# Spectral and gated mix on one core: first loads on one queue, shorter warm-up matmuls, and products in another order with PSUM pairs begun by ScalarE

## Chip, cores and metric

The kernel runs on one core of one Trainium2 chip. The metric is the device time of one execution in microseconds (us). The kernel before took 802.03 us, the median of three runs (801.37 to 802.43).

TensorE (PE) does the matmuls, VectorE (DVE) and ScalarE (ACT) the elementwise work. SyncE (SP) issues loads and GpSimd (POOL) issues stores; each issues on a DMA queue of its own, and the transfers of all queues share the core's 16 DMA engines. PSUM, the memory that TensorE writes into, is used as 8 banks of 128 x 512 fp32; a pair of banks holds one product of 128 x 1024.

## What is computed

```python
x = A_x                                               # (1, 2048, 512), fp32
g = sigmoid((x * gate_w).sum(-1, keepdims=True))
a  = einsum("ts,bse->bte", Cr, x @ Wr.T) - einsum("ts,bse->bte", Ci, x @ Wi.T)   # FNet
gate, up = x @ W_gate, x @ W_up                       # to 1792 columns
b  = (gate * (gate > 0) * up) @ W_down                # ReGLU
return g * a + (1 - g) * b
```

`Cr` and `Ci` (2048 x 2048) and `Wr` and `Wi` (512 x 512) are the real and imaginary parts of Fourier matrices. They come as inputs and are multiplied like any others.

## The kernel before

**Products.** Every large product is cut into 2 x 2 blocks and done with seven block products instead of eight, after Strassen. `LEFT` and `RIGHT` (lines 25 to 28) say which sums of blocks each of the seven multiplies, `ORDER` (29) in which order, and `BANK` (30) in which pair of PSUM banks. fp32 operands are split into a high and a low part in fp32r, so each block product is three matmuls per slice of 128: low by high, high by low, high by high (`PARTS`, 375). `hi_of` (398, ScalarE) makes a high part (the profile's casts into `ch`, `lh`, `xh`), `lo_of` (401, VectorE) the low one (`cl`, `ll`, `xl`).

**Stages, in TensorE's order.**
- Warm-up matmuls (950 to 958): 8 of 128 x 512 on a constant tile.
- `Direct` (544): the first block of gate and up, 96 matmuls in eight plain products, fed as its first loads land.
- 11 gated blocks, `Block` (491): gate and up for two of F's 128-column tiles and half of the rows. Seven products of 12 matmuls, in two banks of 6 each: 84.
- 4 `SpectralBlock`s (655) of 84 for x by Wr and Wi, two for each half of the rows, then two more gated blocks (the tail).
- Rounds (`Round`, 766) into the tiles named `z`: 2 of `Down` (843; 294 matmuls each) for W_down, and 4 of `Sequence` (865; 336 each) for Cr and Ci, of which the last is `Last` (904).

That makes 3456 matmuls after the warm-ups, nearly all of 512 columns. Intermediate results go to DRAM and come back: `hd` (gated blocks, stored by `h_out` with the sums that the next stage needs), `ad` (spectral blocks), `vd` and `zd` (rounds), `lb` (the prepared left operands of ci's two rounds), `wb` (the weights of c = 1, kept for the tail).

**What sets the order of the work.** The class `Plan` (129). Each piece of work is recorded with a key, counted in matmuls of the stream: `op(plan.now - 90, load, ...)` asks for something 90 matmuls before the current place. `due` (182) works out by when each step must be done, `order` (196) then places the steps greedily on each engine: TensorE, SyncE and GpSimd in the order of their keys, VectorE and ScalarE by due time, no sooner than 40 keys ahead (`AHEAD`, 139). `run` (262) maps every buffer onto one of 51 SBUF units of 4 KB per partition (`UNITS`); a unit is given again when its last reader is done, so a new buffer can make its first writer wait for an engine or a store that has nothing else to do with it. PSUM tiles come from a rotation of 8 single banks (`bank`, 336; `Pair`, 339), and a new tile waits for all users of the eighth before it. All instructions are issued by line 126 (`Step.run`), so the trace has that one line for all and groups are told apart by tile names.

**The evacuation of a gated block** (`Block.evac`, 515). After each bank: product 5 is copied by ScalarE from pair a into `t`; VectorE adds product 2 (pair b) to `t`, then subtracts `t` from product 1 (pair c). Products 3 and 4 accumulate onto pairs a and b, which still hold 5 and 2: ScalarE's relu of the first bank into `g`, VectorE's product with the second into `h`. Products 6 and 7 accumulate further; VectorE adds `t` to each bank (`u`), and one scalar_tensor_tensor makes max(u, 0) times the other. `SpectralBlock.evac` (680) has the same form without the relu. A round evacuates by `Round.evac` (811), which copies products 1 and 5 (`u`, `n5`) and then combines banks on VectorE (`w`, `u2`).

**The start** (960 to 988). `Direct` needs half of x's tile 11 and half of its weights `wf` for its first product. The weights (two tiles in two halves, 256 KB each) are issued by SyncE (`load`), x's four halves of 256 KB by ScalarE (`side`, 366); the other x tiles and the weights of c = 1 follow on SyncE. `x_split` and `w_split` make the high and low parts of each half.

**The last round.** `Last.prepare` (907) multiplies the earlier partial result `z` by the gate, adds it to `v` and stores it to `vd`, four times, 24 keys apart, with 8 loads and 4 stores of 512 KB. It begins 150 keys after the second of the four sequence rounds began (`start`, 1063). `Last.end` (935) scales the last product's banks by the gate, adds them to `v` and stores each bank.

**The loads of a sequence round** (`Sequence.rights`, 874): for each quarter jj four tiles `r` of 512 KB from cr or ci, asked for 90 keys before their first use; sums of them in place; then `split` (786) casts them into `ch` and `cl`, 31 and 24 keys ahead of the product.

Of the kernel before, what the change touches and what calls it, by code (L numbers as in the profile page):

```python
# [128 lines left out]
class Plan:  # L129
# [30 lines left out]
    def read(self):  # L160
# [3 lines left out]
        seen, banks = {}, []  # L164
        for s in self.steps:
            for refs, writes in ((s.reads, False), (s.writes, True)):
                for r in refs:
                    old = seen.setdefault(r.base, [])
                    for box, x, w in old:
                        if x is not s and (w or writes) and meet(box, r.box):  # L170
                            s.after.add(x)
                    if writes:
                        old[:] = [o for o in old if not within(o[0], r.box)]
                    old.append((r.box, s, writes))
                    if not r.base.uses and r.base.kind == "bank":
                        banks.append(r.base)
                    r.base.uses.append(s)

        for old, new in zip(banks, banks[8:]):
            new.uses[0].after.update(x for x in old.uses if x is not new.uses[0])  # L180
# [81 lines left out]
    def run(self, nc, unit, bank):  # L262
# [5 lines left out]
        for b in self.bufs:  # L268
            if b.uses and b.kind in ("unit", "bank"):
# [3 lines left out]
        for n, s in enumerate(self.steps):  # L273
            for b in first.get(n, ()):
                if b.kind == "bank":
                    b.tile = bank(b)
                    continue
# [9 lines left out]
def kernel(ctx: ExitStack, tc, xP, xG, wf, wgu, wd, cr, ci, wri, gw, out):  # L287
# [19 lines left out]
    psum = ctx.enter_context(tc.tile_pool(name="psum", bufs=8, space=PSUM))  # L307
# [28 lines left out]
    def bank(b):  # L336
        return psum.tile([P, N], F32, name=b.name, tag="ps")

    class Pair:


        def __init__(self, name):
            self.name, self.banks = name, None

        def new(self):
            self.banks = [Buf(plan, self.name, [N], kind="bank") for _ in range(2)]

        def __getitem__(self, n):
            return self.banks[n].all
# [15 lines left out]

    def side(o, i):
        plan.scalar.dma_start(o, i)
# [19 lines left out]
    def x_raw(q, m):  # L387

        a, *r = RIGHT[m]
        raw = piece[q, {6: "12", 7: "21"}[m] if m in (6, 7) else a] if not r or m in (6, 7) else buf(f"xs{m}")  # L390
        X[q, m] = buf(f"xh{m}", dtype=F32R), buf(f"xl{m}", dtype=F32R), raw

    def x_sum(q, m):
        a, *r = RIGHT[m]
        if r:
            combine(X[q, m][2].all, piece[q, a].all, piece[q, r[0]].all, r[1])
# [15 lines left out]
    SLOT = {5: 0, 1: 1, 2: 2, 4: 0, 3: 1, 7: 2, 6: 3}  # L412

    class Weights:
        def __init__(self, c):
            self.c = c
            self.raw = [buf(f"wr{i}", [4, 2, P]) for i in range(2)]
            self.sum = [buf(f"ws{i}", [3, 2, P]) for i in range(2)]
# [6 lines left out]
        def a_sum(self, i):  # L425
            r, o = self.raw[i], self.sum[i]
            E().vector.tensor_add(o[:, 0], r[:, 1], r[:, 2])
            E().vector.tensor_add(o[:, 1], r[:, 0], r[:, 1])
            E().vector.tensor_add(o[:, 2], r[:, 0], r[:, 3])
            E().scalar.copy(self.a[i][0].all, o.all)  # L430

        def a_lo(self, i):
            E().vector.tensor_sub(self.a[i][1].all, self.sum[i].all, f32(self.a[i][0].all))

        def b_sum(self, i):
            r = self.raw[i]
            E().vector.tensor_sub(r[:, 2:4], r[:, 2:4], r[:, 0:2])

        def b_hi(self, i):
            E().scalar.copy(self.b[i][0].all, self.raw[i].all)  # L440

        def b_lo(self, i):
            E().vector.tensor_sub(self.b[i][1].all, self.raw[i].all, f32(self.b[i][0].all))
# [11 lines left out]
        def of(self, m, i):  # L455
            return [t[:, SLOT[m]] for t in (self.a if m in (5, 1, 2) else self.b)[i]]

    def w_prep(w, key, ahead=66):
        for i in range(2):
            op(key - ahead + 6 * i, w.load, i)  # L460
            op(key - 36 + 12 * i, w.a_sum, i)
            op(key - 30 + 12 * i, w.a_lo, i)
            op(key + 6 * i, w.b_sum, i)
            op(key + 6 * i, w.b_hi, i)
        op(key + 6, w.b_lo, 0)
        op(key + 12, w.b_lo, 1)
# [24 lines left out]
    class Block:  # L491


        def __init__(self, q, w):
            self.q, self.w = q, w
            self.t, self.g, self.u = buf("t"), buf("g"), buf("u")
            self.h = [buf(f"h{d}") for d in range(2)]
            self.ps = {k: Pair("c") for k in "abc"}
            for m in ORDER:
                for i in range(2):  # L500
                    pe(6, self.product, m, i)
                    self.evac(m, i, plan.now)
            h_out(q, w.c, self.h, plan.now + (8 if plan.now > 270 else 100))

        def product(self, m, i):
            w, x, ps = self.w.of(m, i), X[self.q, m], self.ps[BANK[m]]
            if m in (5, 2, 1) and i == 0:
                ps.new()
            n = 0
            for k in range(2):  # L510
                for a, b in PARTS:
                    mm(ps[i], w[a][:, k], x[b][:, k], start=m in (5, 2, 1) and n == 0, stop=n == 5)
                    n += 1

        def evac(self, m, i, key):
            a, b, c = (self.ps[k] for k in "abc")
            t, g, h = self.t, self.g, self.h

            def go():
                e = E()  # L520
                if m == 5:
                    e.scalar.copy(t[:, i], a[i])
                elif m == 2:
                    e.vector.tensor_add(t[:, i], t[:, i], b[i])
                elif m == 1:
                    e.vector.tensor_sub(t[:, i], c[i], t[:, i])

                elif m in (3, 4):
                    j, ps = (0, a) if m == 3 else (1, b)
                    if i == 0:  # L530
                        e.scalar.activation(g[:, j], ps[0], AF.Relu)
                    else:
                        e.vector.tensor_mul(h[0][:, 1] if m == 3 else h[1][:, 0], g[:, j], ps[1])
                else:
                    j, ps, o = (0, a, h[1][:, 1]) if m == 6 else (1, b, h[0][:, 0])
                    u = self.u[:, j] if i == 0 else o
                    e.vector.tensor_add(u, ps[i], t[:, i])
                    if i:
                        e.vector.scalar_tensor_tensor(o, self.u[:, j], 0.0, o, op0=OP.max, op1=OP.mult)

            op(key, go)


    class Direct:
        def __init__(self):
# [6 lines left out]
            self.ps = {(f, j): Pair("c") for f in range(2) for j in range(2)}  # L552
# [17 lines left out]
        def products(self, all):  # L570
            for d, i, f, j, k, n in all:
                first = d == k == n == 0
                if first and i == 0:
                    self.ps[f, j].new()
# [4 lines left out]
        def w_load(self, d, k=slice(0, 2)):  # L579
            load(self.raw[d][:, k], wf[d, :, k])  # L580

        def w_split(self, d, k=slice(0, 2)):
            hi, lo = self.w[d]
            E().scalar.copy(hi[:, k], self.raw[d][:, k])
            E().vector.tensor_sub(lo[:, k], self.raw[d][:, k], f32(hi[:, k]))
# [51 lines left out]
    class Spectral:  # L637
# [8 lines left out]
        def prep(self, m, key):  # L646
            a, *r = LEFT[m]
            raw = self.raw[a] if not r or m in (6, 7) else buf(f"vs{m}")
            w = self.w[m] = buf(f"vh{m}", dtype=F32R), buf(f"vl{m}", dtype=F32R), raw
            if r:  # L650
                op(key, lambda: combine(raw.all, self.raw[a].all, self.raw[r[0]].all, r[1]))
# [3 lines left out]
    class SpectralBlock:  # L655
        def __init__(self, sp, q, ih):
            self.sp, self.q, self.ih = sp, q, ih
            self.t = buf("t")
            self.o = {b: buf("a" + b, (2, 2, HD)) for b in ("12", "21", "22", "11")}
            self.ps = {k: Pair("a") for k in "abc"}  # L660
            for m in ORDER:
                for i in range(2):
                    pe(6, self.product, m, i)
                    op(plan.now, self.evac, m, i)
                if m in (3, 4, 6, 7):
# [462 lines left out]
```

## Time and profile before

| | kernel before |
|---|---|
| median of three runs | 802.03 us |
| span of the profiled execution | 799.7 us |
| TensorE busy | 790.3 us, 99%, 3464 matmuls |
| weight loads (beside the matmuls) | 652.1 us, 82% |
| VectorE busy | 665.6 us, 83%, 791 instructions |
| ScalarE busy | 329.1 us, 41%, 393 instructions |
| GpSimd busy | 91.7 us, 11%, 146 instructions |
| moved by DMA | 192.79 MB, mean 241 GB/s |

The times come from other executions than the profile, so the span is compared with the span of another profile, and the median with a median. "Busy" is a share of the whole span and says nothing about who waits for whom: that stands in the rows of single waits. In those, "[5.22 <-DMA r<-ci]" means that the engine had been idle for 5.22 us and that a load into a tile r from ci released it. A row of the timeline gives start, duration, engine, operation, the tiles as out<-in, and the sizes; "x4" means that four such instructions in a row are folded together. A row of the windows gives the stretch, then the busy time and instructions of PE, weight loads, VectorE, ScalarE and GpSimd, the granted TensorE clock, the mean busy share of the DMA engines, and GB/s. An engine's name with a q (SPq, POOLq) is its sequencer, where DMAs are issued; the number at the end of a DMA row is the median time from issue to landing.

### The profile page before, as it was taken

The numbers are of one execution on the slowest core, as the hardware profiler recorded it, in microseconds if no ns is written. First come the engines' busy times: TensorE is split into PE (matmuls) and PEld (weight loads), VectorE is DVE, ScalarE is ACT, GpSimd is POOL, SyncE is SP. The second block draws the span as 40 slices with busy tenths as digits, with TensorE's granted clock in tenths as the row PEclk, the third lists the DMA queues.
The fourth block names the chain that finished last, engine by engine and source line by source line (L and its number), as shares of the span: only waits on it lengthen the run. The fifth ranks groups of instructions, "written<-read, shape, count | busy, mean of one in ns | idle before, by whom it ended". The sixth has DMA issues, their size and how long they took to land.

```text
span 799.7 us, 9573 instructions
## 1 busy us (share of the span) xinstructions
PE 790.3 (99%) x3464; PEld 652.1 (82%) x3464; DVE 665.6 (83%) x791; ACT 329.1 (41%) x393; POOL 91.7 (11%) x146
## 2 busy tenths in 40 slices
PE   8999999999999999999999999999999999999997
PEld 7888888888888888888888888888888877888885
DVE  7999977868699466999985799996688849988995
ACT  5533221212133144275665668454334335434530
POOL 0101211111112122111131011001000100010000
PEclk9999999999999999999999999999999999999999
DMA  9514553232547599999899989118899995197424
GB/s 346 219 41 145 183 200 145 92 145 93 197 145 250 198 353 400 416 343 344 291 373 413 409 278 370 72 58 244 267 333 401 344 384 178 40 305 270 153 64 143
DMA packets 55039, 192.79 MB, mean 241 GB/s; under 512 B 6352, under 2 KB 6352, under 8 KB 54992
## 3 DMA queue, kind: packets, MB, share of 16 engines
q1 hardware_dynamic: 35120, 120.87, 41.6%
q0 software_dynamic: 19296, 70.26, 25.2%
q10 hardware_dynamic: 576, 1.05, 0.4%
q8 instruction: 27, 0.44, 0.2%
q14 instruction: 20, 0.16, 0.1%
HBM read 120.85 MB, written 71.31 MB: 240 GB/s over the span
## 4 chain that ended last, share of the span: by engine, by line
PE 91%; DMA 6%; DVE 2%; ACT 0%; issue 0%; SPq 0%; ACTq 0%; DVEq 0%
PE z L126 48%; PE c L126 34%; PE a L126 10%; DMA r<-ci 4%; DMA lb<-lb 1%; DVE cl L126 1%; DMA wf<-wf 1%; DVE r L126 0%; ACT ch L126 0%; DVE v L126 0%; DVE z L126 0%; ACT wf0h L126 0%; SPq L126 0%; ACTq L126 0%; DVEq L126 0%
## 5 line engine op out<-in xcount | busy, mean ns | idle before, releaser
L126 ACT CAST ch<-r 128x1024 fp32r<-128x1024 f32 x112 | 116.1, 1053 | 140.8 <-DVE r L126 54.6
L126 PE MATMUL z<-ch,ll 128*128 128x512 f32 x420 | 163.4, 389 | 0.0
L126 PE MATMUL z<-cl,lh 128*128 128x512 f32 x420 | 163.4, 389 | 0.0
L126 PE MATMUL z<-ch,lh 128*128 128x512 f32 x420 | 163.4, 389 | 0.0
L126 DVE TENSOR_TENSOR cl<-r,ch 128x1024 fp32r<-128x1024 f32 x112 | 134.6, 1221 | 27.4 <-ACT ch L126 20.5
L126 PE MATMUL z<-ch,lb 128*128 128x512 f32 x448 | 138.4, 389 | 0.7 <-ACT ch L126 0.7
L126 PEld LDWEIGHTS z<-ch,lb 128*128 128x128 f32 x448 | 84.1, 188 | 18.4 <-ACT ch L126 1.1
L126 PEld LDWEIGHTS z<-ch,lh 128*128 128x128 f32 x420 | 78.8, 188 | 16.5
L126 PEld LDWEIGHTS z<-ch,ll 128*128 128x128 f32 x420 | 78.8, 188 | 16.3
L126 PEld LDWEIGHTS z<-cl,lh 128*128 128x128 f32 x420 | 78.8, 188 | 16.3
L126 PE MATMUL z<-cl,lb 128*128 128x512 f32 x224 | 87.5, 391 | 1.4 <-DVE cl L126 1.3
L126 DVE TENSOR_TENSOR r<-r,r 128x1024 f32<-128x1024 f32 x64 | 76.5, 1219 | 3.6 <-DMA r<-ci 3.0
L126 DVE TENSOR_TENSOR cl<-hr,ch 128x1024 fp32r<-128x1024 f32 (+1 forms) x56 | 59.9, 1087 | 13.4 <-ACT ch L126 10.8
L126 ACT CAST ch<-hr 128x1024 fp32r<-128x1024 f32 (+1 forms) x56 | 51.3, 941 | 28.4 <-DMA hr<-hd 13.8
L126 PEld LDWEIGHTS z<-cl,lb 128*128 128x128 f32 x224 | 42.0, 188 | 11.3 <-DVE cl L126 2.6
L126 ACT ACTIVATE g<-c 128x512 f32<-128x512 f32 x26 | 15.5, 598 | 66.4 <-PE c L126 66.2
L126 PE MATMUL c<-xh,wb0l 128*128 128x512 f32 x104 | 40.5, 389 | 0.0
L126 PE MATMUL c<-xl,wb0h 128*128 128x512 f32 x104 | 40.5, 389 | 0.0
L126 PE MATMUL c<-xh,wb0h 128*128 128x512 f32 x104 | 40.5, 389 | 0.0
L126 PE MATMUL c<-xh,wb1l 128*128 128x512 f32 x104 | 40.5, 389 | 0.0
L126 PE MATMUL c<-xl,wb1h 128*128 128x512 f32 x104 | 40.5, 389 | 0.0
L126 PE MATMUL c<-xh,wb1h 128*128 128x512 f32 x104 | 40.5, 389 | 0.0
(191 smaller groups left out, 1321.3 us busy)
## 6 DMA issues: line engine op xcount, KB each, us to landing
hr<-hd SPq DMA_DIRECT2D x42, 512.0 KB, 7.4
r<-cr SPq DMA_DIRECT2D x32, 512.0 KB, 5.6
r<-ci SPq DMA_DIRECT2D x32, 512.0 KB, 9.2
hd<-hs POOLq DMA_DIRECT2D x28, 512.0 KB, 4.7
lb<-lb SPq DMA_DIRECT2D x28, 512.0 KB, 12.0
ad<-a POOLq DMA_DIRECT2D x16, 512.0 KB, 6.0
l<-ad SPq DMA_DIRECT2D x16, 512.0 KB, 8.8
wr<-wgu SPq DMA_DIRECT2D x14, 512.0 KB, 5.5
```

Of the source, the lines that this page charges most:

```text
L126: getattr(getattr(nc, self.engine), self.name)(*map(ap, self.a), **{k: ap(x) for k, x in self.k.items()})
```

## The change

**Another form of the seven products** (Winograd's). Its sums are chained, 5 builds on 6's and so on, and the order is now 1 5 6 2 7 3 4. The partial results no longer pass through SBUF and VectorE but stay in PSUM: one PSUM tile of 8 banks is split into four fixed pairs x, y, m and t. Product 1 goes to x. ScalarE copies x into y, and 6 accumulates on that; 2 accumulates on x, 7 on y; ScalarE copies y, negated in the blocks, into t, and 4 accumulates there; 5 begins m, and 3 accumulates on it. Only products 1 and 5 start a pair afresh. In blocks ScalarE also copies m after 5 and y after 6 into SBUF (`s5`, `s6`), and VectorE adds these to pairs of two banks at once (128 x 1024). The rotation of banks is gone, so a pair's next use waits for its own last reader.

**Weights and operands.** The left parts of three of the seven products are now raw blocks (`a_hi` replaces `a_sum`); four sums in `b_sum` replace five. The tail's weights are fetched 140 keys ahead instead of 90.

**Rounds** use the same pairs, in the order 1 5 6 3 7 2 4; `u`, `n5`, `w` and `u2` go, `s5` and `s6` come, and the rows of `Round.evac` become one operation of 1024 columns per pair. The load of the tile r22 is keyed to product 6 less 10 where it was keyed to product 3.

**Start.** `side` is gone: x's halves are issued by SyncE, each ahead of the half of `wf` that belongs with it, and the first of those weight halves is loaded and split in two quarters. The warm-up is 18 matmuls of 256 columns.

**Last round.** `prepare` begins 540 keys after `start` and takes 40 keys per step; `end` has no VectorE step ahead of the last product.

The diff's core:

```diff
-LEFT = {1: ("11", "22", 1), 2: ("21", "22", 1), 3: ("11",), 4: ("22",), 5: ("11", "12", 1),
-        6: ("21", "11", -1), 7: ("12", "22", -1)}
-RIGHT = {1: ("11", "22", 1), 2: ("11",), 3: ("12", "22", -1), 4: ("21", "11", -1), 5: ("22",),
-         6: ("11", "12", 1), 7: ("21", "22", 1)}
-ORDER = (5, 2, 1, 3, 4, 6, 7)
-BANK = {5: "a", 3: "a", 6: "a", 2: "b", 4: "b", 7: "b", 1: "c"}
+LEFT = {1: ("11",), 2: ("12",), 3: ("12", 6, -1), 4: ("22",), 5: ("21", "22", 1), 6: (5, "11", -1), 7: ("11", "21", -1)}
+RIGHT = {1: ("11",), 2: ("21",), 3: ("22",), 4: (6, "21", -1), 5: ("12", "11", -1), 6: ("22", 5, -1), 7: ("22", "12", -1)}
+ORDER = (1, 5, 6, 2, 7, 3, 4)
+BANK = {1: "x", 2: "x", 5: "m", 3: "m", 6: "y", 7: "y", 4: "t"}
+FIRST = (1, 5)
...
+    PAIRS = {k: Pair(n) for n, k in enumerate("xmyt")}
...
-    def side(o, i):
-        plan.scalar.dma_start(o, i)
...
         def evac(self, m, key):
+            x, y, p, t = (PAIRS[k] for k in "xymt")
...
+            def added(r, ps, s):
+                u, h = self.u[r], self.h[int(r[0]) - 1][:, 1]
+                op(key, lambda: e.vector.tensor_add(u.all, ps.all, s.all))
+                op(key + 1, lambda: e.vector.scalar_tensor_tensor(h, u[:, 0], 0.0, u[:, 1], op0=OP.max, op1=OP.mult))
+
+            if m == 1:
+                op(key, lambda: e.scalar.copy(y.all, x.all))
+            elif m in (5, 6):
+                op(key, lambda: e.scalar.copy(self.s[m].all, (p if m == 5 else y).all))
+            elif m == 2:
+                rectified("11", 0, x, 1.0)
+            elif m == 7:
+                op(key, lambda: e.scalar.activation(t.all, y.all, AF.Copy, scale=-1.0))
+                added("22", y, self.s[5])
+            elif m == 3:
+                added("12", p, self.s[6])
+            elif m == 4:
+                rectified("21", 0, t, -1.0)
...
-    ORDER_Z = (1, 3, 5, 7, 6, 2, 4)
+    ORDER_Z = (1, 5, 6, 3, 7, 2, 4)
...
             if x == 1:
+                op(key, lambda: e.scalar.activation(Y, X, AF.Copy, scale=-1.0))
+            elif x in (5, 6):
+                op(key, lambda: e.scalar.copy(s[x].all, M if x == 5 else Y))
+            elif x == 3:
+                op(key, lambda: e.vector.tensor_add(o["12"].all, M, s[6].all))
                 self.done("12", key + 6)
+            elif x == 7:
+                op(key, lambda: e.scalar.copy(T, Y))
+                op(key + 8, lambda: e.vector.tensor_add(o["22"].all, Y, s[5].all))
+                self.done("22", key + 14)
...
-                for b, key in (("11", at[1, jj]), ("22", at[3, jj]), ("12", at[5, jj]), ("21", at[2, jj] - 36)):
+                for b, key in (("11", at[1, jj]), ("12", at[5, jj]), ("22", at[6, jj] - 10), ("21", at[2, jj] - 36)):
...
-                k, z, v = key + 24 * i, buf("z"), buf("v")
+                k, z, v = key + 40 * i, buf("z"), buf("v")
...
-    WARM = 8
-    warm, wp = buf("warm", [N], F32R), Pair("warm")
+    WARM = 18
+    warm = buf("warm", [N // 2], F32R)
...
-    halves = [slice(0, 1), slice(1, 2)]
+    halves, quarters = [slice(0, 1), slice(1, 2)], [slice(0, 2), slice(2, 4)]
     for d, b in ((0, "11"), (1, "21")):
         for k in halves:
-            op(-99, direct.w_load, d, k)
-            op(-99, x_load, 0, b, k, side)
+            op(-99, x_load, 0, b, k)
+            for n in quarters if d == k.start == 0 else [slice(0, 4)]:
+                op(-99, direct.w_load, d, k, n)
...
-                    w.fetch(plan.now - 90)
+                    w.fetch(plan.now - 140)
...
-            Last(lefts[m], m, p).prepare(start + 150)
+            Last(lefts[m], m, p).prepare(start + 540)
```

More of the change, by code (lines that the diff above doesn't have):

```diff
@@ L260, in order, with run @@
         self.steps = sorted(done, key=lambda s: s.start)
-    def run(self, nc, unit, bank):
+    def run(self, nc, unit):
         self.read()
@@ L268, in run @@
         for b in self.bufs:
-            if b.uses and b.kind in ("unit", "bank"):
+            if b.uses and b.kind == "unit":
                 first.setdefault(min(at[s] for s in b.uses), []).append(b)
@@ L334, in unit, with __init__, all, __getitem__ @@
         return pool.tile([P, *b.shape], b.dtype, name=b.name, tag=f"u{n}")
-    def bank(b):
-        return psum.tile([P, N], F32, name=b.name, tag="ps")
+    ps8 = Buf(plan, "ps", [8, N], kind="fixed", tile=psum.tile([P, 8, N], F32, name="ps"))
     class Pair:
[L342 to L349, printed above, removed]
+        def __init__(self, n):
+            self.n = 2 * n
+        @property
+        def all(self):
+            return ps8[:, self.n:self.n + 2]
+        def __getitem__(self, i):
+            return ps8[:, self.n + i]
+    PAIRS = {k: Pair(n) for n, k in enumerate("xmyt")}
     def E():
@@ L1069 @@
         else:
[L1070 to L1072 removed]
+            Last(lefts[m], m, p).prepare(start + 540)
+    plan.run(nc, unit)
 _OUT = (1, S, D)
```

241 lines of the change are left out of this document (93 added, 148 removed).

## Prediction

> **What bounds the kernel now.** I read the page's head and the chain first, then who made TensorE wait, then the timeline where it waits, and the windows by stage.
>
> ```profile
> span 799.7 us, 9573 instructions
> ...
> PE 790.3 (99%) x3464; PEld 652.1 (82%) x3464; DVE 665.6 (83%) x791; ACT 329.1 (41%) x393; POOL 91.7 (11%) x146
> ...
> PE 91%; DMA 6%; DVE 2%; ACT 0%; issue 0%; SPq 0%; ACTq 0%; DVEq 0%
> ```
>
> ```profile
> PE warm L126 <- DVE gs L126: 1.5, 1, 1.5
> PE z L126 <- DVE cl L126: 1.3, 2, 0.8
> PE z L126 <- ACT ch L126: 0.7, 1, 0.7
> PE c L126 <- ACT wf0h L126: 0.6, 1, 0.6
> ```
>
> TensorE is busy for 99% of the span and holds 91% of the chain, and its waits are only those four lines. So the number of matmuls times their spacing sets the time, and an edit can win only at the start, at the tail, in stalls, or where matmuls run slowly. The start:
>
> ```profile
> 1.45 3.78 PE L126 MATMUL warm<-warm 128*128 128x512 f32 x8 [1.45 <-DVE gs L126]
> ...
> 5.10 0.62 ACT L126 CAST wf0h<-wf 128x512 fp32r<-128x512 f32 x1 [1.20 <-DMA wf<-wf]
> ...
> 5.85 2.05 PE L126 MATMUL c<-xb11h,wf0h 128*128 128x512 f32 x4 [0.62 <-ACT wf0h L126]
> ...
> 7.69 1.91 PE L126 MATMUL c<-xb11l,wf0h 128*128 128x512 f32 x4
> ...
> 9.40 1.17 PE L126 MATMUL c<-xb11h,wf0l 128*128 128x512 f32 x4
> ```
>
> ```profile
> 29.47 0.39 PE L126 MATMUL c<-xb22h,wa0l 128*128 128x512 f32 x1
> ...
> 353.15 0.39 PE L126 MATMUL z<-ch,ll 128*128 128x512 f32 x1
> ...
> 794.12 0.39 PE L126 MATMUL z<-ch,lb 128*128 128x512 f32 x1
> ```
>
> The matmul at 29.47 is the 97th after the warm-ups, that at 353.15 the 1525th (13 gated blocks and 4 spectral ones of 84 each lie between), that at 794.12 the last, the 3456th (3464 less 8). From 29.47 to 353.15 the spacing is 323.68/1428 = 0.2267 us: nothing is lost there, although VectorE is 83% busy. The first 96 should take 96 x 0.2267 = 21.76 and took 29.47 - 5.85 = 23.62: **1.86 us** lost. The rows at 7.69 and 9.40 say how: groups of four start 1.84 and 1.71 apart instead of 0.91, half rate, until about 9.5, some 3.7 us after the products began. The 1931 steps after 353.15 should take 437.7 and took 440.97: **3.27 us** lost, almost all here:
>
> ```profile
> 652.12 1.05 ACT L126 CAST ch<-r 128x1024 fp32r<-128x1024 f32 x1 [5.22 <-DMA r<-ci]
> ...
> 653.22 0.50 PE L126 MATMUL z<-ch,lb 128*128 128x512 f32 x1 [0.71 <-ACT ch L126]
> ...
> 654.48 0.50 PE L126 MATMUL z<-cl,lb 128*128 128x512 f32 x1 [0.76 <-DVE cl L126]
> ...
> 654.82 0.63 PE L126 MATMUL z<-ch,lb 128*128 128x512 f32 x2
> ...
> 665.47 0.61 PE L126 MATMUL z<-ch,lb 128*128 128x512 f32 x2
> 666.61 0.50 PE L126 MATMUL z<-cl,lb 128*128 128x512 f32 x1 [0.52 <-DVE cl L126]
> ```
>
> ScalarE's cast waits 5.22 us for a load, and TensorE waits behind it. The windows and the issues of that sequence round (563 to 639) show why the load was late:
>
> ```profile
> 563.00:639.00 76.00, 76.00 (x337) 62.90 (x337) 61.93 (x58) 28.32 (x31) 5.59 (x8) 1.00 0.97 338
> ...
> 668.00:716.00 48.00, 48.00 (x214) 39.74 (x213) 46.33 (x43) 21.96 (x24) 2.55 (x3) 1.00 0.49 144
> ```
>
> ```profile
> r<-ci SPq DMA_DIRECT2D x6, 512.0 KB, 16.2
> ```
>
> The DMA engines are 0.97 busy there and a load takes 16.2 us to land; 40 us later they are 0.49 busy.
>
> **The change part by part.** The number and shape of the 3456 products stay, so their 3455 x 0.2267 = 783.1 us stay.
>
> *First loads.* Today x comes by ScalarE's queue beside the weights on SP's, and the first product needs 256 KB of each. Now one queue carries x's 256 KB, then two weight quarters of 128 KB.
>
> ```profile
> 1.40:2.40 1.00, 0.95 (x2) 0.83 (x3) 0.04 (x1) 0.00 (x0) 0.00 (x0) 1.00 0.45 111
> 2.40:3.40 1.00, 1.00 (x4) 0.73 (x3) 0.00 (x0) 0.78 (x1) 0.00 (x0) 1.00 0.98 240
> 3.40:4.40 1.00, 1.00 (x4) 0.81 (x3) 0.00 (x0) 0.50 (x1) 0.00 (x0) 1.00 0.72 244
> ```
>
> ```profile
> 0.74 1.80 SPq L126 DMA_DIRECT2D wf<-wf  x4
> ```
>
> At 244 GB/s the 128 KB no longer in front are worth 0.54 us, and the cast of 256 columns instead of 512 some 0.2 (0.62 for 512 and 1.05 for 1024 give about 0.40 for 256). Against that the quarter is now the second issue on its queue, up to 0.45 us later (1.80 for four). The first product then starts between 5.1 and 5.6; I take **5.3** for 5.85. ScalarE, now free of DMA issues, does its table load earlier, which nothing waits for.
>
> *Warm-ups.* 18 of 256 columns, at half of 3.78/8 = 0.47 each, make 4.2 us, from about 1.2 (the memset of half the columns takes half of its 0.5) to 5.4: no gap before the first product, where today 0.62 us are idle. If 3.7 us of unbroken work bring the full rate, it comes at 4.9 and the 1.86 go; if the run has to start afresh, none do. I take **0.3 us** left. [...]
>
> *Products 1 5 6 2 7 3 4 in pairs of banks.* Counting instructions of the two built programs, VectorE loses 197 of 512 columns and gains 34 of 1024 and 16 of 256; ScalarE gains 109 of 1024 and loses 85 of 512.
>
> ```profile
> L126 DVE TENSOR_TENSOR u<-c,t 128x512 f32<-128x512 f32 x26 | 17.9, 687 | 2.6 <-PE c L126 2.4
> L126 DVE TENSOR_TENSOR ws<-wr 128x256 f32<-128x256 f32 x42 | 15.3, 419 | 0.0
> L126 ACT COPY t<-c 128x512 f32<-128x512 f32 x26 | 15.3, 588 | 59.5 <-PE c L126 59.5
> ...
> L126 DVE TENSOR_TENSOR r<-r,r 128x1024 f32<-128x1024 f32 x64 | 76.5, 1219 | 3.6 <-DMA r<-ci 3.0
> L126 ACT CAST ch<-r 128x1024 fp32r<-128x1024 f32 x112 | 116.1, 1053 | 140.8 <-DVE r L126 54.6
> ```
>
> That is -135 + 41 + 7 = -87 us for VectorE and +115 - 50 = +65 for ScalarE, all beside TensorE, worth nothing by itself. What matters is the new waits. In each of the 17 blocks x is copied into y, s6 is read from y, and -y is copied into t, each with one product of 12 x 0.2267 = 2.72 us before the pair is used. A reader starts some 0.20 us into that product (the last matmul's 0.39, less its own step), a copy of 1024 columns takes 1.03 (588 for 512 plus the cast's step from 0.62 to 1.05), and TensorE follows 0.05 after its releaser (653.17 to 653.22): 1.28 of 2.72, hidden, even behind one cast of 1.05. If the cover is gone, each microsecond ScalarE is late beyond that stops TensorE as long, plus 0.11 for the slow restart (654.48 to 654.82).
>
> In seven of the 17 blocks the built program puts VectorE's read of y first and lets ScalarE's copy of -y wait for it: 0.20 + 1.22 + 0.03 + 1.03 + 0.05 = 2.53 of 2.72. It fits by 0.19. No row shows a copy from PSUM into PSUM: it lies between 1.03 and, if reading and writing share the port, 2.0; I take 1.03, the row nearest in kind. [...]
>
> *Stores that ScalarE now waits for.* In the third spectral block its queue holds, ahead of the copy of -y, the cast of a block that is loaded back after the block before stored it:
>
> ```profile
> ad<-a POOLq DMA_DIRECT2D x4, 512.0 KB, 4.5
> l<-ad SPq DMA_DIRECT2D x4, 512.0 KB, 5.9
> ```
>
> ```profile
> l<-ad SPq DMA_DIRECT2D x16, 512.0 KB, 8.8
> ```
>
> Counted from the end of the spectral block before: copy out 1.3, store 4.5 to 6, load 5.9 to 8.8, then cast, copy of x and copy of -y, 1.05 each and pipelined to 3.0: 14.7 to 19.1, against 6 x 2.72 = 16.3. Behind it in the queue a second cast waits for another such store. Cost 0 to 2.8; I take **0.8** for the spectral blocks, nearer the quick end, since these windows hold 4.5 and 5.9.
>
> *Preparation of the last round*, 8 loads and 4 stores of 512 KB (6.3 MB, 19 us at that window's 338 GB/s), leaves the crowded round from 563 for the quiet stretch from about 672. Then the crowded round has some 25 MB less 6.3 to move, and the late loads come early: of 3.27 us I leave **0.3**. Next late would be VectorE after 680 (46.33 busy of 48.00 in the second window, minus 2 us of evacuation per round now on ScalarE, plus 8 x 1.22 of preparation, spread over the following round).
>
> *Tail.*
>
> ```profile
> 793.19 0.69 DVE L126 TENSOR_TENSOR z<-z,gg 128x512 f32<-128x512 f32 x1 [5.71 <-PE z L126]
> ...
> 794.64 1.69 SPq L126 DMA_DIRECT2D out<-v  x2
> 795.27 0.69 DVE L126 TENSOR_TENSOR v<-v,z 128x512 f32<-128x512 f32 x1
> ```
>
> The same four VectorE operations and two stores follow the last product; only work ahead of them goes. From the last matmul's start to the end it stays 799.7 - 794.12 = 5.6.
>
> Sum: 5.3 + 783.1 + 0.3 + 0.8 + 0.3 + 5.6 = **795.4** for 799.7, 4.3 less. The median shown, 802.03, lies 2.3 above the span; so 802.03 - 4.3 = **797.7**.
>
> **The rivals.** *The start wins nothing*: one queue brings nothing sooner (5.85 again) and the half rate lasts 3.7 us from the first product (1.86 again). For it: 3.78 us of warm-ups did not end it. Against: the 0.62 gap. 797.7 + 0.55 + 1.56 = 799.8.
>
> *ScalarE's queue hangs on stores* in the spectral and following blocks: 2.8 instead of 0.8, and once more behind the 14 stores of lb, which ScalarE's unit reuse now waits for. For it: the rows above. Against: today's windows lost nothing. 797.7 + 3 = 800.7.
>
> *The DMA queue stays late* around 650 although preparation moved: 3.27 stays, 800.7. For it: 25 MB less 6.3 are still 250 GB/s. Against: nothing above half load follows.
>
> *Slower: the copy from PSUM to PSUM costs 2.0 us.* In the seven blocks the chain is then 3.50, 0.78 over, 0.89 with the restart, 6.2 in all: 803.9. Above 1.22 us it begins to cost; above 1.7 the gain is eaten. For it: no row; against: 588 ns per bank from PSUM.
>
> **How the numbers follow.** Forecast 797.7: 0.48, its own range 795.8 to 799.2. Start 0.16, ScalarE's queue 0.16, DMA 0.07, slower copy 0.13. The range, 795.8 to 801.5, leaves out most of the last and the ends of the others. A measurement here tells about 0.2% (1.6 us) from no change: faster 0.70 (the forecast, nearly all of the start, a third of the queue and of the DMA), same 0.15, slower 0.15.
>
> **What would show it.** The first product's start (5.3), groups of four 0.91 apart from there; no TensorE wait on a copy in PSUM; copies of 1024 at 1.03 us; no idle time of TensorE behind `ch` or `cl` around 650; loads of `ci` landing below 10 us. TensorE waiting for ScalarE in gated blocks, or a half rate to 9 us, would make it wrong.

## The result, and the profile after

The changed kernel takes 806.59 us (median of four runs, 805.16 to 808.67) against 801.7 us for the kernel before (its three runs and a fourth, 799.53 to 802.43): ratio 1.0072, 95% interval 1.0051 to 1.0094. It is **slower by 0.7%**, where 797.7 us and a gain were forecast. Its profiled execution has a span of 803.4 us and took 805.16 us, the lowest of its four, so the profile shows the least that was lost.

The head of the page of the changed kernel, then what TensorE waited for in it:

```profile
span 803.4 us, 9431 instructions
...
PE 791.2 (98%) x3474; PEld 653.5 (81%) x3474; DVE 587.8 (73%) x644; ACT 387.5 (48%) x419; POOL 92.1 (11%) x146
```

```profile
PE ps L125 <- ACT ps L125: 2.7, 2, 2.4
PE ps L125 <- DVE cl L125: 2.7, 1, 2.7
PE ps L125 <- DVE gs L125: 1.2, 1, 1.2
PE ps L125 <- ACT s L125: 0.5, 1, 0.5
```

VectorE is 78 us less busy and ScalarE 58 more (87 and 65 were counted), and the 3456 products are there (3474 less 18). What differs is who waits: the waits behind `ch` around 650 are gone; three behind ScalarE's copies and one of 2.7 us behind `cl` are new. TensorE's timeline at the start, at the 97th product and at the last:

```profile
1.19 4.21 PE L125 MATMUL ps<-warm 128*128 128x256 f32 x18 [1.19 <-DVE gs L125]
5.19 1.46 PE L125 MATMUL ps<-xb11h,wf0h 128*128 128x512 f32 x4
6.49 1.09 PE L125 MATMUL ps<-xb11l,wf0h 128*128 128x512 f32 x4
...
27.43 0.39 PE L125 MATMUL ps<-xb11h,wa0l 128*128 128x512 f32 x1
...
797.80 0.39 PE L125 MATMUL ps<-ch,lb 128*128 128x512 f32 x1
```

From the 97th product to the last there are 3359 steps of 323.68/1428 = 0.2267 us, 761.4. The changed kernel took 797.80 - 27.43 = 770.4: 9.0 lost; the kernel before lost 3.3 (764.65 less 761.4). The start is 2.04 us ahead (27.43 for 29.47), the tail the same (5.6). So the profile's 3.7 us more are -2.0 at the start and +5.7 behind it, nearly all in two places.

**The spectral blocks, 300 to 315: 3.9 us.** TensorE, then ScalarE's queue:

```profile
300.06 0.50 PE L125 MATMUL ps<-vh,xl 128*128 128x512 f32 x1 [0.26 <-ACT ps L125]
...
306.28 0.50 PE L125 MATMUL ps<-vh,xl 128*128 128x512 f32 x1 [0.49 <-ACT s L125]
...
311.62 0.39 PE L125 MATMUL ps<-vh,xh 128*128 128x512 f32 x1
314.41 0.50 PE L125 MATMUL ps<-vh,xl 128*128 128x512 f32 x1 [2.40 <-ACT ps L125]
```

```profile
297.12 1.05 ACT L125 CAST lh<-l 128x1024 fp32r<-128x1024 f32 x1 [5.67 <-DMA ad<-a]
298.08 1.01 ACT L125 COPY a<-ps 128x1024 f32<-128x1024 f32 x1
298.99 1.02 ACT L125 COPY ps<-ps 128x1024 f32<-128x1024 f32 x1
...
305.21 1.01 ACT L125 COPY s<-ps 128x1024 f32<-128x1024 f32 x1 [1.54 <-DMA lb<-lh]
309.88 1.02 ACT L125 COPY a<-ps 128x1024 f32<-128x1024 f32 x1 [3.65 <-DMA lb<-ll]
312.40 1.04 ACT L125 CAST lh<-lr 128x1024 fp32r<-128x1024 f32 x1 [1.51 <-DMA lb<-lh]
313.35 1.01 ACT L125 ACTIVATE ps<-ps 128x1024 f32<-128x1024 f32 x1
```

Each releaser in this second fence is a *store*, and of a tile that has nothing to do with the instruction: `a` has no use for `lb<-ll`. What the two share is the SBUF unit: the planner gave it to the new buffer (to `s` the unit of an `lh`, to `a` that of an `ll`), and the store of the old one had not landed. The copies inside PSUM that TensorE needs (298.99, 313.35) wait for nothing themselves; they stand behind such writers in the queue. The copy into `s` at 305.21, behind which TensorE waits 0.49 us, is such a writer itself.

**The third sequence round, 709 to 719: 4.6 us.** TensorE, VectorE and the granted clock:

```profile
711.59 0.61 PE L125 MATMUL ps<-ch,lb 128*128 128x512 f32 x2
714.87 0.50 PE L125 MATMUL ps<-cl,lb 128*128 128x512 f32 x1 [2.66 <-DVE cl L125]
...
716.72 0.63 PE L125 MATMUL ps<-cl,lb 128*128 128x512 f32 x1
717.14 1.05 PE L125 MATMUL ps<-ch,lb 128*128 128x512 f32 x2
718.00 0.63 PE L125 MATMUL ps<-cl,lb 128*128 128x512 f32 x1
```

```profile
713.59 1.22 DVE L125 TENSOR_TENSOR cl<-r,ch 128x1024 fp32r<-128x1024 f32 x1 [3.30 <-DMA vd<-v]
```

```profile
712.00:714.00 2.00, 0.21 (x1) 0.00 (x0) 0.41 (x1) 1.99 (x3) 0.29 (x1) 1.00 1.02 397
...
716.00:718.00 2.00, 2.00 (x7) 1.53 (x5) 2.00 (x2) 0.00 (x0) 0.56 (x1) 0.50 1.05 272
```

`cl` waits 3.30 us for the store of `v`, the moved preparation's, whose unit it takes over. The DMA engines are full (1.02). Of the 4.6 us, 3.0 are the wait and its restart. The other 1.6 follow from 715.9 to 719.3, where three matmuls take 1.28 us (716.72 to 718.00) instead of 0.68, at a granted clock of 0.50.

### The profile page after: what moved, and what is told of

Same layout as the page of the kernel before. It is cut to its first block, busy times and chain, and to the rows that moved or that the text cites. A ratio compares the mean times of both kernels' runs of the same rounds, so it can differ in the third digit from the quotient of the medians.

```text
span 803.4 us, 9431 instructions
## 1 busy us (share of the span) xinstructions
PE 791.2 (98%) x3474; PEld 653.5 (81%) x3474; DVE 587.8 (73%) x644; ACT 387.5 (48%) x419; POOL 92.1 (11%) x146
## 4 chain that ended last, share of the span: by engine, by line
PE 83%; issue 10%; DMA 4%; POOL 2%; DVE 1%; ACT 0%; POOLq 0%; ACTq 0%; DVEq 0%
PE ps L125 83%; DMA lb<-lh 1%; DMA vd<-v 1%; DMA ad<-a 1%; POOL ad L125 1%; POOL hd L125 1%; DVE z L125 0%; POOL z L125 0%; DVE h L125 0%; DVE v L125 0%; DVE u L125 0%; DVE cl L125 0%; ACT a L125 0%; ACT ps L125 0%; DVE hs L125 0%
## 5 line engine op out<-in xcount | busy, mean ns | idle before, releaser
L125 PE MATMUL ps<-ch,ll 128*128 128x512 f32 x420 | 163.4, 389 | 0.0
L125 PE MATMUL ps<-cl,lh 128*128 128x512 f32 x420 | 163.4, 389 | 0.0
L125 PE MATMUL ps<-ch,lh 128*128 128x512 f32 x420 | 163.4, 389 | 0.0
L125 PE MATMUL ps<-ch,lb 128*128 128x512 f32 x448 | 139.5, 392 | 0.0
L125 PEld LDWEIGHTS ps<-ch,lb 128*128 128x128 f32 x448 | 84.8, 189 | 17.8
L125 PEld LDWEIGHTS ps<-ch,ll 128*128 128x128 f32 x420 | 78.8, 188 | 16.5
L125 PEld LDWEIGHTS ps<-cl,lh 128*128 128x128 f32 x420 | 78.8, 188 | 16.3
L125 PEld LDWEIGHTS ps<-ch,lh 128*128 128x128 f32 x420 | 78.8, 188 | 16.3
L125 PE MATMUL ps<-cl,lb 128*128 128x512 f32 x224 | 87.9, 392 | 2.7 <-DVE cl L125 2.7
L125 ACT COPY s<-ps 128x1024 f32<-128x1024 f32 x42 | 42.6, 1014 | 56.5 <-PE ps L125 54.1
L125 DVE TENSOR_TENSOR u<-ps,s 128x1024 f32<-128x1024 f32 x26 | 31.4, 1219 | 15.6 <-PE ps L125 12.9
```

Source lines behind the costliest of these rows:

```text
L125: getattr(getattr(nc, self.engine), self.name)(*map(ap, self.a), **{k: ap(x) for k, x in self.k.items()})
```

## The experiments

**Theory:** two separate losses with one pattern, writers that wait for SBUF units under store: lb's and ad's stores in the spectral blocks, and the preparation's in the third round. **Rivals:** the product order and its PSUM pairs make the copies late by themselves; or the DMA engines are simply full, and whatever needs data is late.

All were timed against the kernel before on the same chips, where it took 800.5 to 801.0 us. "Lost" is what TensorE lost from the 97th product to the last in the profile, reckoned as above. In the expectations the kernel before stands at 801.7; on that scale a ratio r is 801.7 r. Each profile shows one execution, and the times of one kernel spread by up to 5.2 us (the profile of a_left240 took 809.11, its median is 807.61). So the losses say where time goes; what an edit is worth is read from the ratios.

| run | median, us | ratio to before, 95% | 97th at | lost after it: total; where |
|---|---|---|---|---|
| before (first page) | 801.7 | 1 | 29.47 | 3.3; 652 to 667 |
| changed | 806.59 | 1.0072 (1.0051 to 1.0094) | 27.43 | 9.0; 3.9 at 300 to 315, 4.6 at 709 to 719 |
| b_start | 799.57 | 0.9978 (0.9966 to 0.9990) | 27.56 | 3.5; 645 to 665 |
| b_warm | 800.38 | 0.9996 (0.9983 to 1.0009) | 27.91 | 3.7; 645 to 666 |
| a_prep150 | 804.18 | 1.0038 (1.0023 to 1.0053) | 27.89 | 9.2; 4.9 at 300 to 318, 3.9 at 657 to 662 |
| b_prep540 | 801.31 | 1.0005 (0.9992 to 1.0018) | 29.47 | 5.7; 707 to 748 |
| a_prep420 | 803.10 | 1.0039 (1.0026 to 1.0053) | 27.26 | 6.8; 3.2 at 306 to 314, 2.7 at 672 to 676 |
| b_start_prep420 | 801.97 | 1.0016 (1.0004 to 1.0027) | 27.07 | 5.9; 662 to 675 |
| a_left240 | 807.61 | 1.0071 (1.0050 to 1.0091) | 27.50 | 12.9; 1.9 at 346, 2.3 at 429, 7.4 from 711 to 743 |
| a_land9 | 803.27 | 1.0037 (1.0023 to 1.0051) | 27.03 | 9.0; 0.6 at 339, 6.6 at 724 to 738 |
| a_land9_prep420 | 801.77 | 1.0015 (1.0006 to 1.0025) | 27.48 | 5.6; 0.6 at 339, 3.8 at 672 to 684 |
| a_land9_prep150 | 801.15 | 1.0006 (0.9994 to 1.0017) | 27.18 | 5.2; 0.6 at 339, 3.0 at 650 to 656 |
| b_start_land9 | 801.30 | 1.0003 (0.9992 to 1.0014) | 27.60 | 5.5; 3.2 at 648 to 667, rest spread |
| b_start_ahead110 | 798.71 | 0.9970 (0.9958 to 0.9981) | 27.71 | 1.8; 1.2 at 665 to 669 |
| a_land9_prep150_ahead110 | 797.81 | 0.9969 (0.9957 to 0.9980) | 27.89 | 1.8; 0.6 at 340, rest spread |
| **b_start_ahead130** | **797.05** | **0.9956 (0.9944 to 0.9969)** | 27.23 | 0.3 |

### The start alone

b_start is the kernel before with only the part "Start" of the change; b_warm has only its warm-up:

```diff
-    WARM = 8
-    warm, wp = buf("warm", [N], F32R), Pair("warm")
+    WARM = 18
+    warm, wp = buf("warm", [N // 2], F32R), Pair("warm")
```

> The kernel before with only the start of the changed one: one queue, x ahead of the weights, the first weight half in quarters, 18 warm-up matmuls of 256 columns. Theory (the start brings what the changed kernel's trace shows: first product 0.66 us sooner, the 97th matmul 2.04 us sooner, and nothing later gives it back): 2.0 less, 799.7 for 801.7. Rival (a later stall takes it back, since loads due at fixed times are then later by as much): 801.0 to 801.7.

> The kernel before with 18 warm-up matmuls of 256 columns and nothing else of the new start (loads on two queues as before). Theory (the half rate goes because the warm-up has no gap to the first product; the first product's start is set by the loads): first product at 5.85 as before, the 97th matmul 0.9 to 1.5 us sooner, 800.2 to 800.8 for 801.7. Rival (the gain needs the earlier first product, since warm-up of any length must start afresh): the 97th matmul at 29.3 to 29.5, 801.7.

b_start has its 97th product 1.9 us sooner and keeps it. In b_warm the first product comes no sooner, yet the half rate ends early:

```profile
1.19 4.21 PE L126 MATMUL warm<-warm 128*128 128x256 f32 x18 [1.19 <-DVE gs L126]
5.91 1.30 PE L126 MATMUL c<-xb11h,wf0h 128*128 128x512 f32 x4 [0.51 <-DVE xb11h L126]
7.04 1.08 PE L126 MATMUL c<-xb11l,wf0h 128*128 128x512 f32 x4
```

Groups of four are 1.13 and then 0.92 apart, where the kernel before had 1.84 and 1.71. So the warm-up brings 1.56 us in the profile (27.91 for 29.47), the queue and the quarters some 0.7 in the first product's start (5.20 for 5.91). Only the profile shows this gain. The times (0.9983 to 1.0009) reach down to 1.4 us less and don't show any; the 1.56 would be 0.9981, just outside.

### Where the preparation stands

```diff
-                k, z, v = key + 40 * i, buf("z"), buf("v")
+                k, z, v = key + 24 * i, buf("z"), buf("v")
...
-            Last(lefts[m], m, p).prepare(start + 540)
+            Last(lefts[m], m, p).prepare(start + 150)
```

That is a_prep150; b_prep540 is the reverse in the kernel before; a_prep420 and b_start_prep420 have 420 and 24.

> The changed kernel with the preparation of the last round put back to 150 keys after start, 24 keys apart. Theory (the changed kernel's stall of 4.9 us at 709 to 719 comes from that preparation's stores, which hold SBUF units while the DMA engines are full): the stall goes, and TensorE loses nothing between 700 and 730. The crowded sequence round before it gets its 6.3 MB back, so between 0 and the 3.3 us that the kernel before lost at 652 to 667 come with it: 4.9 to 1.6 less than the changed kernel, 801.7 to 805.0 for 806.6. Rival (the stall comes from the new order of products in the rounds and the later load of r22): the stall stays near 710 and up to 3.3 us at 652 are added, 806.6 to 809.9.

> The kernel before with only the preparation of the last round moved to 540 keys after start, 40 keys apart. Theory (stores of the preparation hold units in a full DMA): the 3.3 us at 652 to 667 go, and a wait for a store vd<-v, or for a buffer that it holds, appears on VectorE or ScalarE between 695 and 730; what of it reaches TensorE lies between 0 and 4.9: 798.4 to 803.3 for 801.7. Rival (the new product order makes the stall): 3.3 less and no wait of TensorE after 690, 798.4.

In a_prep150 the wait near 710 is gone and the loss at 657 is back:

```profile
657.22 0.50 PE L125 MATMUL ps<-ch,lb 128*128 128x512 f32 x1 [0.98 <-ACT ch L125]
658.48 0.50 PE L125 MATMUL ps<-cl,lb 128*128 128x512 f32 x1 [0.76 <-DVE cl L125]
```

b_prep540 has the old products, loses nothing near 650, and gets the same wait at 710, first VectorE, then TensorE:

```profile
709.75 1.23 DVE L126 TENSOR_TENSOR cl<-r,ch 128x1024 fp32r<-128x1024 f32 x1 [2.74 <-DMA vd<-v]
```

```profile
711.03 0.50 PE L126 MATMUL z<-cl,lb 128*128 128x512 f32 x1 [0.95 <-DVE cl L126]
```

So this wait belongs to the move and not to the products. In the profile 5.7 were lost in all, above the 4.9 that the theory allowed: 1.4 around the wait at 711, 2.4 at 719 to 725, where VectorE waits 1.22 for a load of `v`, and 1.6 at 743 to 748. By its time (802.1 on the scale) the run lies in the theory's range, but it can't be told from the kernel before.

> The changed kernel with the preparation of the last round 420 keys after start, 24 apart: its loads and stores fall at about 650 to 685, behind the crowded round and ahead of the full stretch from 700. Theory (it is the place of those 12 transfers that makes both the loss at 652 to 667 of the kernel before and that at 709 to 719 of the changed one): neither comes, only the spectral 3.9 stay, 802.0 for 806.6, or 803.5 if a part of the crowd at 650 stays. Rival (any place costs as much, since VectorE has no room from 680 on): a loss of 3 to 5 us somewhere after 640, 805 to 807.

> The kernel before with the changed start and with the preparation 420 keys after start, 24 apart, products as before. Theory (start worth 2.0, the place of the preparation worth the 3.3 us at 652 to 667): 796.4 on the scale on which the kernel before has 801.7, ratio 0.993. Rival (VectorE, 97% busy from 668 to 708 in the kernel before, can't take the preparation there and makes TensorE wait): 798 to 801, with waits behind cl between 670 and 720.

a_prep420 comes to 804.8 on the expectations' scale and b_start_prep420 to 803.0, both above the theory's range and nearer to the rivals', the second above that as well. Stores hold up casts of ScalarE (0.52 us at 669.65 in a_prep420, 5.06 at 671.12 in b_start_prep420), but every wait of TensorE there is behind VectorE's `cl`, and VectorE waits for no store in those stretches. It is full from 670 on (9.54 to 10.00 busy of each 10 us to 710 in a_prep420), and `cl` stands behind the preparation's own operations:

```profile
672.02 1.22 DVE L125 TENSOR_TENSOR r<-r,r 128x1024 f32<-128x1024 f32 x1
673.15 1.22 DVE L125 TENSOR_TENSOR v<-v,z 128x1024 f32<-128x1024 f32 x1
674.83 1.23 DVE L125 TENSOR_TENSOR cl<-r,ch 128x1024 fp32r<-128x1024 f32 x1 [0.46 <-issue]
```

With the old products, which load VectorE more (665.6 us busy in the kernel before, 587.8 in the changed one), it is 5.8 instead of 2.7.

### Which stores, and whether it is the queue or the DMA

a_left240 moves the first preparation of ci's left operands out of the spectral blocks:

```diff
-    lefts[1].prep(0, plan.now + 72, 14, lb)
+    lefts[1].prep(0, plan.now + 240, 14, lb)
```

> The changed kernel with the first preparation of ci's left operands (7 sums, 7 casts, 7 low parts, 14 stores to lb) keyed 168 matmuls later, so that it runs beside the two tail blocks instead of the last two spectral ones. Theory (ScalarE's copies out of PSUM are late there because casts and copies ahead of them in its queue wait for SBUF units that stores still hold): the 3.9 us between 300 and 315 go, 802.7 for 806.6, unless the tail blocks, which have the same copies, lose a part of it: up to 806.6. Rival (the copies are late because of the order of products and PSUM pairs alone): the waits at 300, 306 and 314 stay, 806.6.

The waits at 300 to 315 go, as the theory said, but the time does not (807.4 on the scale, above its range): new ones come behind ScalarE at 346 and behind VectorE at 429 and from 711. The DMA share at 300 to 320 fell too (0.67), so this run could not tell a busy queue from a full DMA. a_land9 can: no work is moved by hand, and only the planner is told when a store lands. The 9.0 go by the issuing engine: they hold for all that GpSimd issues, loads added into `z` among them, while SyncE's stores to `out` keep 2.1.

```diff
-                s.end = line + self.LANDING + (2.0 if "accum_op" in s.k else 0)
+                s.end = line + (self.LANDING if s.engine == "sync" else 9.0) + (2.0 if "accum_op" in s.k else 0)
```

> The changed kernel with one number of its planner changed: a store is taken to land 9.0 us after its transfer, not 2.1, as it does in the full stretches of the traces (vd<-v 7.1 to 9.7 us). Loads keep 2.1. No work is moved by hand. Theory (both stalls are waits for SBUF units that the planner gives again while a store from them is still under way): of the 3.9 us at 300 to 315 and the 4.6 at 709 to 719 at most 2.5 stay together, 798 to 801 on the scale on which the changed kernel has 806.6 and the one before 801.7. Rival (the DMA engines are simply full there, and whatever needs data is late): units come free later in the plan, loads are issued later still, and the loss stays or grows: 805 to 810.

The windows of before, of the changed kernel and of a_land9 for 300 to 320 (PE's busy time stands first behind the stretch, the DMA share last but one):

```profile
300.00:320.00 20.00, 20.00 (x90) 16.57 (x89) 13.69 (x16) 8.40 (x11) 5.75 (x10) 1.00 1.02 399
```

```profile
300.00:320.00 20.00, 17.05 (x72) 13.47 (x73) 10.41 (x10) 10.68 (x12) 7.49 (x14) 1.00 1.03 418
```

```profile
300.00:320.00 20.00, 20.00 (x90) 16.53 (x90) 12.08 (x12) 12.44 (x15) 7.02 (x12) 1.00 1.03 418
```

The DMA engines are as full in all three (1.02, 1.03, 1.03); TensorE loses 3 us only in the middle one. ScalarE's queue in a_land9 shows no store as a releaser:

```profile
298.20 1.00 ACT L125 COPY ps<-ps 128x1024 f32<-128x1024 f32 x1 [1.66 <-PE ps L125]
...
309.76 1.02 ACT L125 ACTIVATE ps<-ps 128x1024 f32<-128x1024 f32 x1
```

So the spectral loss is shown: SBUF units under store, in a queue on which TensorE now depends. (The new plan gives other units and also puts both copies inside PSUM, 298.20 and 309.76, ahead of the casts that stood before them; what each of the two saves was not tried alone.) With 804.7 on the scale the run is far above the theory's 798 to 801 and close to the rival's 805, for in the third round the theory **fails**. One wait for a store is left there, 3.24 us of ScalarE at 711.27 behind a store to `out`, and TensorE loses nothing by it; yet 6.6 us are lost at 724 to 738. TensorE waits behind `cl`, and before that VectorE for loads of `r` (1.19 and 1.32 us):

```profile
724.72 1.23 DVE L125 TENSOR_TENSOR r<-r,r 128x1024 f32<-128x1024 f32 x1 [1.19 <-DMA r<-ci]
...
728.40 1.23 DVE L125 TENSOR_TENSOR r<-r,r 128x1024 f32<-128x1024 f32 x1 [1.32 <-DMA r<-ci]
...
733.57 0.50 PE L125 MATMUL ps<-cl,lb 128*128 128x512 f32 x1 [3.43 <-DVE cl L125]
```

The nine loads of `r` issued between 700 and 735 take 14.2 us to land (median). So the preparation's traffic in that stretch looks too much, whichever transfer is late: there the second rival fits, though no run with the preparation at 540 asked for those loads sooner.

### Repairs together, and loads asked for sooner

> Both repairs together: the changed kernel with stores taken to land after 9.0 us in the plan, and with the preparation of the last round 420 keys after start, its 40 keys per step kept so that VectorE's extra operations don't come in one bunch. Theory (two separate losses, spectral stores 3.9 and the preparation's place 4.6): the first falls to the 0.6 that the 9 us alone left, the second to between 0 and the 2.7 that 420 with steps of 24 left: 806.6 less 5.2 to 7.9, 798.7 to 801.4, ratio to the kernel before 0.996 to 1.000. Rival (the room between the two full stretches is too small for the preparation, wherever it is): a loss of 4 to 6 us after 640 stays, 803 to 805.

> The changed kernel with stores taken to land after 9.0 us in the plan, and the preparation where the kernel before has it (150 keys after start, steps of 24). Theory (new products in PSUM pairs are worth nothing either way once the spectral stores are out of the way, and the crowded round costs 3.3 to 3.9 again): the kernel before less the start's 2.0, plus 0.6 for each: 799.7 to 800.9. Rival (the PSUM copies cost time in other places too): 803 or more.

> The kernel before with the new start and with stores taken to land after 9.0 us in the plan. Theory (units given again too soon cost time where ScalarE or VectorE must serve TensorE at once; the kernel before lost nothing in the spectral blocks, and its 3.3 us at 652 to 667 come from loads that are late, not stores): no gain beyond the start, 799.0 to 800.5. Rival (the planner's landing time is the cause of the loss at 652 as well): 3.3 less, 796.4.

Both repaired kernels come near the one before, at 802.9 and 802.2 on the scale, 1.3 us or more above the theory's ranges and below the rivals', the first by only 0.1. Wherever the preparation stands, 3.0 to 3.8 us stay. In b_start the 9 us do nothing for the loss at 650 and lose some 2 us in small waits elsewhere, so that loss is not about stores, as expected; the small waits were not expected, and the time (801.9) lies above its range. The loss is the lateness of loads:

```diff
-                    op(key - 90, lambda r=r, b=b, jj=jj: load(
+                    op(key - 130, lambda r=r, b=b, jj=jj: load(
```

> The kernel before with the new start, and with the tiles r of the sequence rounds asked for 110 matmuls before their first use instead of 90 (4.5 us sooner). Theory (the loss at 645 to 667 comes from loads of ci that land 10 to 16 us after their issue, and SBUF has units for asking sooner): the 3.3 us shrink to 0 to 1.5, 796.3 to 797.8 on the scale on which the kernel before has 801.7. Rival (the DMA engines are full for the whole round, so asking sooner only lengthens the queue, or units for the tiles come free no sooner): 799.0 to 800.5, or worse if the tiles take units that other work needs.

> As the run with 110, but 130 ahead (9.1 us sooner). Theory: no loss at 645 to 667, 796.3 to 797. Rival: as there, 799 to 802, with waits in new places where units are short.

> The changed kernel with stores taken to land after 9.0 us, the preparation of the last round where the kernel before has it, and the tiles r asked for 110 ahead. Theory (of its 5.2 us lost after the start, 3.0 at 650 to 656 come from late loads): 797.5 to 799. Rival (asking sooner in a full round brings nothing): 800.5 to 801.5.

On the scale these are 799.3, 798.2 and 799.2, each somewhat above the theory's range, and by its time alone the first lies in the rival's; but the profiles show what was asked, 3.5 us lost with 90, 1.8 with 110 and 0.3 with 130, and the same with the new products (5.2 and 1.8). In b_start_ahead130 TensorE waits for nothing after the warm-up's start; its list of waits has one line, and the stretch that lost 2.1 us now loses none, in a DMA as busy (0.92 before, 0.91):

```profile
PE warm L126 <- DVE gs L126: 1.2, 1, 1.2
```

```profile
639.00:668.00 29.00, 26.89 (x115) 21.08 (x114) 17.27 (x17) 11.39 (x12) 0.84 (x1) 1.00 0.92 340
```

```profile
639.00:668.00 29.00, 29.00 (x130) 24.02 (x129) 22.01 (x20) 10.67 (x12) 0.00 (x0) 1.00 0.91 342
```

The first of these rows is the kernel before, the second b_start_ahead130: the DMA engines move no more (342 GB/s for 340), the loads were only asked for 9 us sooner. This kernel beats the one before by 0.4% and, by the ratios to it, the changed one by 1.2%.

## Why the prediction was wrong

- **The start: right.** Forecast 5.3 + 21.76 + 0.3, the 97th product at 27.36; measured 27.43. That they meet within 0.07 is partly luck: in the 14 profiles with 18 warm-ups that product starts at 27.03 to 27.91. The reason given for the half rate was partly wrong: that there is no gap before the first product is not what counts, since b_warm has one of 0.5 us and loses 0.24. What of the longer warm-up (4.21 us for 3.78) or its earlier start (1.19 for 1.45) decides was not tried. The 0.3 left for the half rate was a choice between 0 and 1.86, and no run shows that term by itself; in its place the 14 profiles lost 0.23 to 0.94 in the first 96 products. Nor is all of that half rate: in a_land9 and b_start_prep420 the full rate came before the first product (4.73 and 4.79), and each still lost 0.5 in gaps a few us later. The kernel before starts its warm-ups at 1.45, and its products run at half rate until about 9.4; whether its gap of 0.62 us is the reason was not tried.
- **The products in the gated blocks: right.** Only 0.2 us are lost from 27.43 to 299 in the changed kernel. Copies from PSUM to PSUM take 1.0 us, so the rival that made it slower did not come about:

```profile
L125 ACT COPY ps<-ps 128x1024 f32<-128x1024 f32 x23 | 23.0, 999 | 59.6 <-PE ps L125 39.6 <-DVE z L125 20.0
```

- **"Stores that ScalarE now waits for", 0.8 of 0 to 2.8: failed**, with 3.9. The place and the queue were right, the mechanism was not. The prediction followed one block of data out and back (store, load, cast); the runs show the SBUF units, which any store holds, and 11 of lb and six of `a` were issued between 283 and 318 in the changed kernel. The rival "ScalarE's queue hangs on stores" named unit reuse, at 3 us and a chance of 0.16.
- **"Preparation of the last round", 0.3 left: failed**, with 4.6. The crowded round did lose nothing any more, but the quiet stretch was none. The row 668 to 716 (0.49) was an average over two halves. In windows of 8 us the kernel before shows:

```profile
676.00:684.00 8.00, 8.00 (x37) 6.60 (x36) 7.93 (x8) 3.96 (x4) 0.00 (x0) 1.00 0.17 60
684.00:692.00 8.00, 8.00 (x37) 6.63 (x36) 7.96 (x8) 5.19 (x6) 0.00 (x0) 1.00 0.01 2
692.00:700.00 8.00, 8.00 (x37) 6.64 (x36) 7.93 (x10) 2.78 (x4) 0.85 (x1) 1.00 0.34 110
700.00:708.00 8.00, 8.00 (x37) 6.60 (x37) 7.94 (x9) 3.31 (x5) 0.85 (x1) 1.00 0.97 228
708.00:716.00 8.00, 8.00 (x37) 6.64 (x36) 6.80 (x6) 2.47 (x4) 0.84 (x1) 1.00 1.04 330
```

From 700 on the DMA engines were full already, and 540 keys with steps of 40 put three of the four stores of `v` there (703.78, 716.25 and one later). That VectorE would be the next limit from 680 was said, and shown by a_prep420.
- **The tail: right**, 5.6 us.
- The sum: 795.4 forecast, 803.4 measured; 3.1 more in the spectral blocks, 4.3 more at the preparation, 0.6 in small losses and the start. The range reached to 801.5 since each of these was weighed alone; two together left it.

What stays open: why the other three runs of the changed kernel took 1.4 to 3.5 us longer than the profiled one, and what makes the small losses of the runs with 9.0 us (with the new products 0.6 at 339 and 0.7 at 86 to 91 in all four, where the changed kernel itself loses nothing). With the 9.0 us, the old place of the preparation and the loads 110 ahead, the new products (0.9969) are no better than the old ones with 110 (0.9970): TensorE sets the time, and here relief for VectorE bought nothing.

## What to carry to other kernels

When an edit makes the bounding engine depend on another engine's queue, read that queue for every buffer that its instructions write and ask who held the memory last; a store that has not landed stops it like a missing input (here a copy of ScalarE waited 3.65 us behind a store of `ll`, and a cast of the kernel before 5.22 us for a load). Before work is moved into a quiet stretch, cut the stretch into windows as short as the work itself. A load that is late in a full DMA may only need to be asked for sooner (here a stretch that lost 2.1 us at a DMA share of 0.92 lost none at 0.91).

## What the hardware showed unexpectedly

A wait of TensorE can cost more than its length. After the wait of 2.66 us that ended at 714.87 the rate was halved from 715.9 to 719.3, 1.6 us more, with 0.50 granted at 716 to 718. (At the start the same column shows 1.00 in the stretches quoted in the prediction, though the matmuls run at half rate there: eight warm-ups of 512 columns take 3.78 us, 0.47 each, against 0.2267.) In a_prep150 waits of 0.98 and 0.76 us had the same effect:

```profile
659.91 1.05 PE L125 MATMUL ps<-ch,lb 128*128 128x512 f32 x2
660.77 0.63 PE L125 MATMUL ps<-cl,lb 128*128 128x512 f32 x1
661.19 1.05 PE L125 MATMUL ps<-ch,lb 128*128 128x512 f32 x2
```

But the wait of 2.40 us that ended at 314.41 in the changed kernel had none: the next matmuls are 0.24 apart. The same wait in a_prep150, 2.32 us to 314.44, had one, from 315.0 to 317.6, which cost 1.2 us and accounts for its 4.9 lost there against 3.9. So the half rate followed waits of 0.98 and 0.76 us, of 2.32 and of 2.66 us, and did not follow one of 2.40 us; what decides is not shown.
